# Loading the first slice of wq from ScalarE's queue, beside the first load of x

## The chip, the cores and the metric

The kernel runs on one core of a Trainium2 chip. Times are device microseconds (us) of one execution. The profile's "span", from the first to the last instruction, is in most runs 1.7 to 2.1 us shorter than that time. One of the first three runs of the kernel before took 343.19 us; it is a slow run and enters no comparison. TensorE is PE in the profile (PEld is its weight load), VectorE is DVE, ScalarE ACT, GpSimd POOL, SyncE SP; a q after a name is that engine's queue, which issues DMAs.

## The reference, cut to what matters

```python
x = A_x                                        # 2048 tokens x 640, bf16
g = sigmoid((x * gate_w).sum(-1, keepdims=True))
a = linear_attention(x @ wqkv, ...) @ wo       # 32 heads, phi(q), phi(k), sums over tokens
b = shift_mlp_block(x, w1, w2, w3, w4)
out = g * a + (1 - g) * b
```

Only the very beginning is touched by the change: x and the q columns of `A_wqkv` (called wq, 640 x 640) come in from memory, x is transposed, and the first four tiles of q are computed.

## The kernel before: the parts that matter

wq is cut into five slices of 128 rows (160 KB each), one per step of the contraction. Every load of the start-up is on SyncE, in this order:

```python
dma_in(x_tok[:, 0:2, :], ..., "x01")           # 320 KB: tokens 0-255
dma_in(x_tok[:, 2:4, :], ..., "x23")           # 320 KB: tokens 256-511
for k in range(KD):                            # KD = 5
    load_wq(k)                                 # 160 KB each
for k in range(KD):
    dma_in(wkg[:, k, 0:D], ..., "wk%d" % k)
...                                            # gate weights, the rest of x
```

TensorE begins with matmuls on a tile of ones, which do nothing but keep it at work, then transposes x, then streams q through four tiles:

```python
NWARM = 5
NWARM2 = 2
...
addA(("warm",), 0.0, lambda: warmup(NWARM, 427.0))
for i in range(4):
    addA(("tx", i), 0.28, lambda i=i: t_x(i))  # 5 transposes of one x tile, copied to xT
    if i % 2:
        addA(("warm", i), 0.0, lambda: warmup(NWARM2, 300.0))
addA(("q", 3), 5.44, q_four)                   # needs wq slice 0 first, then 1, 2, ...
addA(("k", 0), 1.36, k_first)
```

A helper works out all waits from what each operation reads and writes; each engine then runs its own list in order.

## Time and profile before

| | before |
|---|---|
| time, median of three runs | 267.33 us (fast runs 266.66 and 267.33) |
| span of the profiled run | 265.2 us |
| TensorE busy | 260.8 us, 98% |
| first x transposes start | 3.92 us |
| first wq matmul starts | 7.28 us |

The page's busy line of TensorE, and the engines of the chain of waits that ended last:

```profile
PE 260.8 (98%) x1729; PEld 137.3 (52%) x1729; DVE 146.3 (55%) x242; ACT 107.9 (41%) x218; POOL 91.8 (35%) x148
...
PE 98%; DVE 0%; POOL 0%; issue 0%; POOLq 0%
```

TensorE is both the busiest engine and the chain. The waits view of TensorE (engine, line, releaser; us in total, times, longest) has a single entry in the whole run, the start itself:

```profile
engine line waited for: us in total, times, longest us
PE ps L831 <- POOL ones_c L665: 1.6, 1, 1.6
```

The start-up in the timeline (start, duration, engine, line, operation, tiles, count, and in brackets the idle time before it with what ended it):

```profile
0.79 1.28 ACT L662 ACT_TABLE_LOAD   x1 [0.79 <-PEq L1226]
...
0.80 0.96 SPq L283 DMA_DIRECT2D x_tok<-in_A_x_dram  x2
...
1.59 2.31 PE L831 MATMUL ps<-ones_c 128*128 128x512 bf16 x5 [1.59 <-POOL ones_c L665]
...
1.81 2.36 SPq L283 DMA_DIRECT2D wq<-in_A_wqkv_dram  x5
...
3.91 0.99 PEld L617 LDWEIGHTS ps<-ident,x_tok 128*128 128x128 bf16 x10 [0.92 <-DMA x_tok<-in_A_x_dram]
3.92 1.25 PE L617 MATMUL ps<-ident,x_tok 128*128 128x128 bf16 x10
...
4.96 1.06 PE L831 MATMUL ps<-ones_c 128*128 128x512 bf16 x2
...
6.85 0.59 PE L831 MATMUL ps<-ones_c 128*128 128x512 bf16 x2
...
7.28 0.38 PE L853 MATMUL ps<-wq,xT 128*128 128x512 bf16 x1
```

SyncE issues the two x loads from 0.80 and the wq slices from 1.81. The warm-up matmuls end at 3.90, the transposes start at 3.92, and their weight loads waited for x_tok until 3.91: the first x load lands just there. The first wq matmul comes at 7.28, behind transposes and two more pairs of warm-up matmuls. wq slice 0 was issued at 1.81 and landed 3.7 to 3.9 us later (the range of the five slices in the source view), near 5.6, so it had over 1.5 us to spare.

The clock of TensorE shows in the weight loads and in the matmuls: the pair of warm-up matmuls at 4.96 takes 1.06 us, the same pair at 6.85 takes 0.59; single weight loads take 0.15 us before and 0.10 after. The switch from slow to full is at about 6.9 us. The page's row of granted clock does not show it; it is 9 everywhere.

Packets of the DMA queues between 1.8 and 3.4 us (packets, MB, share of the 16 engines' time). The first x load has 256 rows of 1280 bytes, and by the packet counts of these queues 16 more small packets at its end, 272 in all; wq slice 0 has 128 + 16 = 144:

```profile
q1 hardware_dynamic: 313, 0.38, 89.3%
```

By 3.4 us more packets have passed than the first x load has. (The 16 engines are not in step, so a few of them belong to the second.)

### The profile page before, as it was taken

The numbers are of one execution on the slowest core, as the hardware profiler recorded it, in microseconds if no ns is written. First come the engines' busy times: TensorE is split into PE (matmuls) and PEld (weight loads), VectorE is DVE, ScalarE is ACT, GpSimd is POOL, SyncE is SP. The second block draws the span as 40 slices with busy tenths as digits, with TensorE's granted clock in tenths as the row PEclk, the third lists the DMA queues.
The fourth block names the chain that finished last, engine by engine and source line by source line (L and its number), as shares of the span: only waits on it lengthen the run. The fifth ranks groups of instructions, "written<-read, shape, count | busy, mean of one in ns | idle before, by whom it ended". The sixth has DMA issues, their size and how long they took to land.

```text
span 265.2 us, 4339 instructions
## 1 busy us (share of the span) xinstructions
PE 260.8 (98%) x1729; PEld 137.3 (52%) x1729; DVE 146.3 (55%) x242; ACT 107.9 (41%) x218; POOL 91.8 (35%) x148
## 2 busy tenths in 40 slices
PE   7999999999999999999999999999999999999995
PEld 4555555555555555554445545545454455545553
DVE  0487877899903797999786986321212121122232
ACT  2486767742365757775651211212321312121000
POOL 4003995859874025688820204000120011021020
PEclk9999999999999999999999999999999999999999
DMA  7675899543568995256466831120000200002011
GB/s 224 221 100 140 184 175 150 174 102 22 104 124 114 304 371 70 48 99 64 63 124 124 103 68 30 31 95 2 0 0 6 95 0 0 2 0 101 0 49 49
DMA packets 50355, 24.77 MB, mean 93 GB/s; under 512 B 41756, under 2 KB 48925, under 8 KB 50336
## 3 DMA queue, kind: packets, MB, share of 16 engines
q1 hardware_dynamic: 49184, 21.23, 37.6%
q0 software_dynamic: 1152, 3.28, 5.4%
q8 instruction: 13, 0.21, 0.3%
q14 instruction: 6, 0.05, 0.1%
HBM read 12.04 MB, written 2.62 MB: 55 GB/s over the span
## 4 chain that ended last, share of the span: by engine, by line
PE 98%; DVE 0%; POOL 0%; issue 0%; POOLq 0%
PE ps L606 61%; PE ps L1100 21%; PE ps L783 8%; PE ps L853 2%; PE ps L831 1%; PE ps L1082 1%; PE ps L1022 1%; PE ps L617 1%; PE ps L939 1%; PE ps L854 1%; DVE x_tok L645 0%; POOL ones_c L665 0%; POOLq L1226 0%
## 5 line engine op out<-in xcount | busy, mean ns | idle before, releaser
L662 ACT ACTIVATE h2T<-ps 128x512 bf16<-128x512 f32 x52 | 31.0, 597 | 83.8 <-PE ps L606 83.7
L606 PE MATMUL ps<-xnT,w_58 128*128 128x512 bf16 x260 | 60.9, 379 | 0.0
L1100 PE MATMUL ps<-w_84,h2T 128*128 128x512 bf16 (+1 forms) x416 | 58.8, 299 | 0.0
L628 POOL TENSOR_SCALAR abx<-x_tok,stg 128x640 f32<-128x640 bf16 x16 | 13.9, 874 | 107.4 <-DVE x_tok L645 71.2
L1100 PEld LDWEIGHTS ps<-w_84,h2T 128*128 128x128 bf16 x416 | 32.7, 98 | 27.8 <-issue 1.3
L645 DVE SCALAR_TENSOR_TENSOR x_tok<-ps,stg,abx 128x640 bf16<-128x640 f32 (+2 forms) x17 | 14.3, 844 | 51.7 <-PE ps L1100 51.7
L606 PEld LDWEIGHTS ps<-xnT,w_58 128*128 128x128 bf16 x260 | 24.1, 98 | 24.8 <-issue 1.0
L645 DVE SCALAR_TENSOR_TENSOR abx<-ps,stg,abx 128x640 f32<-128x640 f32 x16 | 14.1, 882 | 27.9 <-PE ps L606 24.9
L662 ACT ACTIVATE Er<-ps 128x640 bf16<-128x640 f32 x32 | 22.4, 704 | 13.7 <-PE ps L606 8.8
L662 ACT ACTIVATE hsT<-ps 128x512 bf16<-128x512 f32 (+1 forms) x32 | 18.9, 593 | 14.6 <-PE ps L606 14.3
L661 ACT ACTIVATE junk<-x_tok 128x640 bf16<-128x640 bf16 x32 | 23.6, 736 | 2.0 <-DVE x_tok L643 1.7
L606 PE MATMUL ps<-M_sb,pqnT 128*128 128x512 bf16 (+1 forms) x160 | 24.1, 299 | 0.0
L606 PE MATMUL ps<-xnT,w_59 128*128 128x512 bf16 x100 | 23.9, 379 | 0.0
L783 PE MATMUL ps<-pk_tok,x_tok 128*128 128x512 bf16 (+1 forms) x160 | 23.9, 299 | 0.0
L606 PE MATMUL ps<-w_60,hsT 128*128 128x512 bf16 (+1 forms) x160 | 23.7, 299 | 0.0
L606 PE MATMUL ps<-wkg,xT 128*128 128x512 bf16 (+1 forms) x150 | 22.6, 299 | 0.0
L606 PEld LDWEIGHTS ps<-w_60,hsT 128*128 128x128 bf16 x160 | 13.3, 98 | 12.1
L606 PEld LDWEIGHTS ps<-M_sb,pqnT 128*128 128x128 bf16 x160 | 13.2, 98 | 12.1 <-issue 0.6
L628 POOL TENSOR_SCALAR xn<-x_tok,st_54 128x640 bf16<-128x640 bf16 x16 | 17.5, 1097 | 4.5 <-DMA xnT<-xn 4.4
L606 PE MATMUL ps<-wq,xT 128*128 128x512 bf16 (+1 forms) x120 | 18.3, 299 | 0.0
L628 POOL TENSOR_SCALAR xn<-x_tok,st_55 128x640 bf16<-128x640 bf16 x16 | 16.2, 1024 | 5.0 <-DMA xnT<-xn 4.6
L628 DVE TENSOR_SCALAR Er<-Er 128x640 bf16<-128x640 bf16 x32 | 12.0, 375 | 10.3 <-ACT Er L662 10.2
(74 smaller groups left out, 266.9 us busy)
## 6 DMA issues: line engine op xcount, KB each, us to landing
w_58<-in_B_w_dram SPq DMA_DIRECT2D x1, 2160.0 KB, 8.5
w_84<-in_B_w_dram SPq DMA_DIRECT2D x1, 2080.0 KB, 14.1
x_tok<-in_A_x_dram SPq DMA_DIRECT2D x3, 640.0 KB, 5.9
out_dram<-x_tok SPq DMA_DIRECT2D x3, 640.0 KB, 3.3
wq<-in_A_wqkv_dram SPq DMA_DIRECT2D x5, 160.0 KB, 3.8
wkg<-in_A_wqkv_dram SPq DMA_DIRECT2D x5, 160.0 KB, 4.1
wv<-in_A_wqkv_dram POOLq DMA_DIRECT2D x1, 800.0 KB, 5.9
wo_aug<-in_A_wo_dram POOLq DMA_DIRECT2D x5, 150.0 KB, 5.1
```

Of the source, the lines that this page charges most:

```text
L606: ins = e.matmul(out_ap, l, r, start=(i == 0), stop=(i == n - 1))
L617: ins = e.transpose(o, s_, ident[:])
L628: return engf(lambda e: e.tensor_scalar(out_ap, in_ap, s1, s2, op0, op1), rd, [out_ap], cost=cost)
L645: return dve(lambda e: e.scalar_tensor_tensor(out_ap, in0, scalar, in1, op0, op1), rd, [out_ap], cost=cost)
L661: return act(lambda e: e.activation(out_ap, in_ap, func, bias=bias, scale=scale, accum_out=accum), rd, wr, cost=cost)
L662: return act(lambda e: e.activation(out_ap, in_ap, func, bias=bias, scale=scale), rd, wr, cost=cost)
L783: ins = e.matmul(o, l, r, start=(t0 + q_ == 0), stop=(t0 + q_ == NT - 1))
L831: ins = e.matmul(ps[:, b, :], ones_c[:, 0:128], ones_c[:, 128:640], start=True, stop=True)
L853: e.matmul(ps[:, b, 0:512], l, w[:, k, 0:512], start=(k == 0), stop=(k == KD - 1))
L854: return e.matmul(ps[:, b + 1, 0:n2], l, w[:, k, 512:512 + n2], start=(k == 0), stop=(k == KD - 1))
L939: ins = e.matmul(o, l, r_, start=st_, stop=sp_, skip_group_check=True)
L1100: ins = e.matmul(o, l, r, start=False, stop=(i == KFF - 1))
```

## The change

The intent is to have the first wq slice early: its load is given to ScalarE's queue, which is free at the start, beside the first x load. The other slices stay behind x on SyncE.

```diff
+    sch.dma("act", wq[:, 0, :], A_wqkv[0:128, 0:D], "wq0")
     dma_in(x_tok[:, 0:2, :], x2[0:256, :]..., "x01")
...
     dma_in(x_tok[:, 2:4, :], x2[256:512, :]..., "x23")
-    for k in range(KD):
+    for k in range(1, KD):
         load_wq(k)
```

The instruction lists of TensorE, VectorE and GpSimd are the same in both kernels; only the two queues differ.

## The prediction

> **What bounds the kernel now.** TensorE: the page's busy table gives PE 260.8 us of a 265.2 us span (98%), and the chain that ended last is 98% PE. The waits view lists one PE wait in the whole run: 1.6 us for the ones tile of the warm-up matmuls.
>
> In the timeline, five warm-up matmuls end at 3.90. The first x transposes start at 3.92; the weight-load lane waited 0.9 us for the x_tok load until 3.91. This load (x01, 320 KB) is issued at 0.80 and lands after 3.1 us, at 3.9: it lands just as the warm-up ends, with no slack. x23 lands near 4.8 (issued about 1.28, 3.5 us; from the two-load median 3.3), used at 5.39 to 5.81. wq0 is issued at 1.81 and lands 3.7 to 3.9 us later, about 5.6. Its first matmul is at 7.28, right behind transposes and warm-ups in PE order: about 1.6 us of slack. No wait for wq appears.
>
> **What the change does.** It removes one issue (0.43 to 0.48 us) from SyncE, so x23 is unaffected and wq1 onward is issued about 0.48 us earlier. It adds one issue ahead of ScalarE's table load (0.79, 1.28 us long); ScalarE then idles 3.1 us until 5.20, so this is free. Nothing else changes order. wq0 itself should land about 1 to 1.3 us earlier (near 4.4), which nobody was waiting for: worth 0.
>
> The cost: wq0 now starts beside x01. The Trainium skill, "DMA: Bandwidth & Descriptors", section "Issuing engines are not separate DMA queues", says both queues end on the same 16 engines and interleave. The DMA view agrees that there is no spare room: share 84% from 1.59 to 3.92, then about 100% at 333 to 350 GB/s. wq0's 160 KB at 350 GB/s is 0.47 us. x01 has twice wq0's bytes, so with fair alternation x01 finishes after all or most of wq0: x01 lands an estimated 0.3 to 0.5 us later, 4.2 to 4.4. PE gets a gap of about 0.4 us before the first transposes. x23 moves as much, still before its use.
>
> **What of it is critical.** All of that gap, less one thing. PE runs at half clock until about 6.9 (weight loads 152 ns, later 98; warm-ups 427 ns apart, then 215). If the clock rises at a fixed time, as the skill's "TensorE: Matmul & The Clock Gate", Part 1, describes (a free-running activity window of about 3.4 us), work pushed past 6.9 runs twice as fast: a 0.4 us gap costs an estimated 0.2 us. If the rise slides with the gap, it costs 0.4; if the gap spoils a window, up to 1.7 (half of 3.4).
>
> **Predicted.** Fast runs of before are 266.66 to 267.33. I expect +0.1 to +0.5 us, +0.25 central: 267.35 us, 8 in 10 between 266.6 and 268.4. Faster by over 2%: 0.01; within 2%: 0.97; slower by over 2%: 0.02.
>
> **What would show it.** (1) First x transposes start 0.3 to 0.5 us later, with a PE wait on the x_tok load. (2) wq0 lands at 4.2 to 4.6, 1 us or more before its first matmul. (3) First wq matmul at 7.4 to 7.8. (4) Table load starts later by about 0.5, the first ScalarE copy still waits for PE. (5) Then a constant shift to the end; no new PE wait.
>
> **What would make it wrong.** ScalarE's queue starts late, so x01 goes first undisturbed: no change. The descriptor generation of both queues is shared and x01 waits longer: +0.5 or more. The clock rise moves by a whole window: -1 to +1.7 us. Run-to-run spread (0.7 us) exceeds the effect.

## The result, and the profile after

| | before | after |
|---|---|---|
| median of 6 runs | 267.0 us (the slow one among them; the five fast runs 266.66 to 267.33) | 268.53 us (267.95 to 269.51) |
| span of the profiled run | 265.2 us | 266.8 us |
| first x transposes start | 3.92 us | 4.68 us |
| clock of TensorE rises, by the weight loads | 6.9 us | 9.3 us |

The ratio is 1.0061, 95% interval 1.0039 to 1.0084. Ratios here are the mean time of one kernel's fast runs over that of the other's in the same rounds, so they are not quite the ratio of the medians. The kernel became 0.6% slower, about 1.6 us: still "the same" at 2%, but clear of noise, and above the range of the prediction.

The page's lines again, and TensorE's waits:

```profile
PE 261.6 (98%) x1729; PEld 137.5 (52%) x1729; DVE 145.7 (55%) x242; ACT 107.9 (40%) x218; POOL 91.7 (34%) x148
...
PE 97%; DMA 1%; DVE 0%; issue 0%
```

```profile
PE ps L832 <- POOL ones_c L665: 1.6, 1, 1.6
PE ps L617 <- DMA x_tok<-in_A_x_dram: 0.8, 1, 0.8
```

A second wait has come: 0.8 us for x. The DMA is now part of the chain. The timeline:

```profile
0.79 0.42 ACTq L283 DMA_DIRECT2D wq<-in_A_wqkv_dram  x1
...
0.80 0.97 SPq L283 DMA_DIRECT2D x_tok<-in_A_x_dram  x2
1.24 1.28 ACT L662 ACT_TABLE_LOAD   x1 [1.24 <-PEq L1227]
...
1.59 2.31 PE L832 MATMUL ps<-ones_c 128*128 128x512 bf16 x5 [1.59 <-POOL ones_c L665]
...
4.67 0.98 PEld L617 LDWEIGHTS ps<-ident,x_tok 128*128 128x128 bf16 x10 [1.68 <-DMA x_tok<-in_A_x_dram]
4.68 1.25 PE L617 MATMUL ps<-ident,x_tok 128*128 128x128 bf16 x10 [0.78 <-DMA x_tok<-in_A_x_dram]
...
8.49 0.63 PE L854 MATMUL ps<-wq,xT 128*128 128x512 bf16 x1
...
9.03 0.15 PEld L855 LDWEIGHTS ps<-wq,xT 128*128 128x128 bf16 x1
...
9.38 0.10 PEld L854 LDWEIGHTS ps<-wq,xT 128*128 128x128 bf16 x1 [0.20 <-issue]
```

The lines answer to those of before. ScalarE issues wq0 at 0.79, a hair before SyncE's x at 0.80; its table load slips from 0.79 to 1.24, which nobody feels. The warm-up ends at 3.90 as before, but x lands later: transposes at 4.68. The first wq matmul moves from 7.28 to 8.49. And the clock rises late: weight loads are still 0.15 us at 9.03 and 0.10 from 9.38.

The DMA queues between 1.8 and 3.4 us:

```profile
q10 hardware_dynamic: 141, 0.16, 60.3%
q1 hardware_dynamic: 111, 0.14, 24.7%
```

Queue 10 is ScalarE's. It has moved 141 of wq0's 144 packets by 3.4 us. SyncE's queue has moved 111, where it had moved 313 before; together the two queues moved 61 packets fewer than the one queue before, about 0.2 us of work at the 64 packets per 0.2 us of the kernel before near 3 us. These two counts could still come from turn-taking. The start decides it. From 1.8 to 2.2 us queue 10 alone moved packets (39), and from 2.2 to 2.6:

```profile
q10 hardware_dynamic: 27, 0.03, 48.9%
q1 hardware_dynamic: 8, 0.01, 10.6%
```

That is 66 against 8. The later overlap is one of engines that are not in step. The packed trace holds the small packet that ends each engine's share of a load: taken in order, x's came 0.68 us after wq0's on 14 of the 16 engines. At the 0.052 us per packet of e7_cols (0.834 us for 16 rows there) this is 13 of x's 16 rows per engine; turns of one row each would have left 8. So wq0 mostly went first. It landed 3.1 us after its issue, at 3.9 us, and was then used at 8.49.

**Where the 1.6 us come from.** Until the rise TensorE works at half speed (in the chain of waits two warm-up matmuls count 0.85 us before it and 0.43 after). So a delay in that stretch costs half its length, and each microsecond by which the rise comes later costs half a microsecond. Starting useful work 4.68 - 3.92 = 0.76 us later costs 0.38 us; the rise 9.3 - 6.9 = 2.4 us later costs 1.2 us. Together 1.58 us, against 266.8 - 265.2 = 1.6 us of span. From there on the run is only shifted: the group of three k tiles starts at 15.70 in place of 14.09, the first wo load is issued at 50.1 in place of 48.5, the last store at 264.4 in place of 262.8, each 1.6 us later.

So there are two questions: why x came 0.76 us late and not the expected 0.3 to 0.5, and whether the gap caused the late rise or the late rise was chance.

### The profile page after: what moved, and what is told of

Its sections match the earlier page's. It is cut to its first block, busy times and chain, and to the rows that moved or that the text cites. A ratio compares the mean times of both kernels' runs of the same rounds, so it can differ in the third digit from the quotient of the medians.

```text
span 266.8 us, 4339 instructions
## 1 busy us (share of the span) xinstructions
PE 261.6 (98%) x1729; PEld 137.5 (52%) x1729; DVE 145.7 (55%) x242; ACT 107.9 (40%) x218; POOL 91.7 (34%) x148
## 4 chain that ended last, share of the span: by engine, by line
PE 97%; DMA 1%; DVE 0%; issue 0%
PE ps L606 61%; PE ps L1101 21%; PE ps L784 8%; PE ps L854 2%; DMA x_tok<-in_A_x_dram 1%; PE ps L1083 1%; PE ps L1023 1%; PE ps L617 1%; PE ps L832 1%; PE ps L940 1%; PE ps L855 1%; DVE x_tok L645 0%
## 5 line engine op out<-in xcount | busy, mean ns | idle before, releaser
L628 POOL TENSOR_SCALAR xn<-x_tok,st_54 128x640 bf16<-128x640 bf16 x16 | 17.5, 1095 | 6.9 <-DMA xnT<-xn 6.8
L628 POOL TENSOR_SCALAR xn<-x_tok,st_55 128x640 bf16<-128x640 bf16 x16 | 16.8, 1058 | 5.1 <-DMA xnT<-xn 4.6
```

Source lines behind the costliest of these rows:

```text
L628: return engf(lambda e: e.tensor_scalar(out_ap, in_ap, s1, s2, op0, op1), rd, [out_ap], cost=cost)
```

## The experiments

Main theory: (1) wq0, issued first, goes ahead of x in the DMA engines; (2) the gap that this leaves in TensorE's work puts off the rise of its clock, which costs more than the gap. Rivals: the late rise is a chance of phase (of how the timing of the clock happens to stand when the kernel starts); the second queue costs by itself, through the table load or through sharing; only bytes count.

Twelve runs were made, of eleven kernels (e10 is e4 once more), all with correct results. Their times are set against the kernel before in the same session, whose own median is given, because it differs a little from session to session.

| kernel | median, before in that session | ratio, 95% interval | first x transposes start |
|---|---|---|---|
| three warm-up matmuls (e1_gap) | 267.98, 267.13 | 1.0029, 1.0008 to 1.005 | 3.90 |
| changed, seven warm-up matmuls (e2_fill) | 266.87, 267.13 | 0.9999, 0.9978 to 1.0019 | 4.89 |
| changed, wq0 issued at 2.68 (e3_late) | 266.91, 267.13 | 0.9991, 0.9973 to 1.0009 | 3.80 |
| wq0 first on SyncE (e4_spfirst) | 267.58, 267.13 | 1.0022, 0.999 to 1.0054 | 4.82 |
| before, dummy of 16 KB on ScalarE (e5_small) | 267.36, 266.77 | 1.0025, 1.0006 to 1.0043 | 4.22 |
| changed, 64 rows on ScalarE (e6_rows) | 266.34, 266.77 | 0.9987, 0.9969 to 1.0005 | 4.15 |
| changed, half rows on ScalarE (e7_cols) | 267.37, 266.77 | 1.0043, 1.0013 to 1.0074 | 4.51 |
| before, no warm-up pairs (e8_lean) | 266.55, 266.77 | 0.9999, 0.9979 to 1.0019 | 4.03 |
| changed, wq0 issued at 1.56 (e9_mid) | 266.7, 266.25 | 1.0022, 0.999 to 1.0053 | 3.77 |
| e4 once more, one look (e10_spagain) | 267.49, 266.25 | none | 4.21 |
| a try at a faster start (e11_try) | 266.85, 266.25 | 1.0018, 0.9986 to 1.005 | 4.74 |
| four warm-up matmuls (e12_gap4) | 266.78, 266.96 | 0.9987, 0.9974 to 1.0 | 3.61 |

### Is it the gap? A gap alone, and the change without its gap

The first takes two dummy matmuls away from the kernel before and leaves all loads as they were. TensorE idles, but nothing useful starts later.

```diff
-    NWARM = 5
+    NWARM = 3
```

> Kernel before with three warm-up matmuls in place of five, queues untouched. TensorE then idles about 0.85 us (3.05 to 3.9) before the first transposes, which start at the same 3.9 as before: no useful matmul is delayed. Main theory (a gap in TensorE's work puts off the rise of its clock): the rise (weight loads going from 0.15 to 0.10 us) moves from 6.9 to 8.5-10, and the span grows by half of that move, +0.8 to +1.5 us. Rival (the later rise in the changed kernel was chance of phase, or came from the DMA traffic): rise stays at 6.9 +- 0.5 and the time is that of before within 0.3 us.

```profile
1.58 1.46 PE L831 MATMUL ps<-ones_c 128*128 128x512 bf16 x3 [1.58 <-POOL ones_c L665]
...
3.90 1.25 PE L617 MATMUL ps<-ident,x_tok 128*128 128x128 bf16 x10 [0.85 <-DMA x_tok<-in_A_x_dram]
...
7.29 0.15 PEld L853 LDWEIGHTS ps<-wq,xT 128*128 128x128 bf16 x1 [0.27 <-issue]
...
7.71 0.10 PEld L854 LDWEIGHTS ps<-wq,xT 128*128 128x128 bf16 x1 [0.28 <-issue]
```

The transposes start at 3.90, as in the kernel before, after a gap of 0.85 us. The weight loads are still slow at 7.29 and fast at 7.71. The time is 1.0029 of before (1.0008 to 1.005), about 0.8 us more, by doing less. In its one profile the span grew by only 0.4 us with the rise near 7.7, 0.8 later: half of the move, as the sum above has it, though less of a move than the 8.5 to 10 expected of it; the other runs' spans go up to 266.7, against 264.4 to 265.8 for the kernel before in that session. A gap of this length costs time that no delayed work explains. (The six times show this, not the one profile: e12_gap4 below had its rise at 7.6 almost without a gap.)

The second keeps the changed loads, with x as late as there, but adds two warm-up matmuls so that TensorE is hardly idle (0.1 us in the profile, from 4.75 to 4.89).

```diff
-    NWARM = 5      # changed kernel
+    NWARM = 7
```

> Changed kernel with seven warm-up matmuls in place of five, so that they last until about 4.75, past the landing of the first x load at 4.63: x is as late, but TensorE has no gap. Main theory: the clock rises near 6.9 again (6.4 to 7.4), the useful chain starts 0.85 us later on the slow clock, and the total is +0.3 to +0.5 us over before, not the +1.6 of the changed kernel. Rival (the gap does not matter): rise near 9.3 and +1.6 us as in the changed kernel.

```profile
1.58 3.17 PE L832 MATMUL ps<-ones_c 128*128 128x512 bf16 x7 [1.58 <-POOL ones_c L665]
...
4.89 0.56 PEld L617 LDWEIGHTS ps<-ident,x_tok 128*128 128x128 bf16 x10 [1.04 <-DMA x_tok<-in_A_x_dram]
...
6.88 0.38 PE L854 MATMUL ps<-wq,xT 128*128 128x512 bf16 x1
```

x landed even later here, and transposes started at 4.89. Yet their ten weight loads took 0.56 us, not 0.99: the clock had risen already by about 4.9, earlier than the 6.4 to 7.4 expected. The time is that of before (0.9999), not the 0.3 to 0.5 us above it that were expected; the 0.43 us that two more slow warm-up matmuls should cost is within the interval. This run and the changed kernel differ in nothing but the filling of the gap, and the 1.6 us are gone: the six spans are 264.8 to 265.7 us here and 266.2 to 267.5 in the changed kernel. Chance of phase, with the gap playing no part, is ruled out by the two runs together.

Phase does play a part, though. The Trainium skill, "TensorE: Matmul & The Clock Gate", Part 1 ("What's actually happening"), says that the clock follows activity in a free-running window of 3413 ns that is not reset when a kernel starts. That agrees with what is seen here: with no gap, the rise was at 6.9 in one profile and before 4.9 in another, and the spans of the kernel before range from 264.0 to 266.1 us over the sessions. If all of this came from the rise, it would be a range of an estimated 4 us in it.

The other profiles bear out the sum by which the 1.6 us were split. Take 265.2 us and add half of what the transposes start later than 3.92 and half of what the rise (read from the spacing of the matmuls, 0.43 us slow and 0.22 fast) comes later than 6.9. For e1_gap (rise 7.7) this gives 265.6 us, e4_spfirst (7.9) 266.1, e5_small (6.9) 265.4, e7_cols (5.3) 264.7, e9_mid (5.7) 264.5, e10_spagain (7.6) 265.7 and e12_gap4 (7.6) 265.4; each measured span is within 0.1 us of it. The rises also sort by the gap: with gaps of at most 0.14 us (seven profiles) they lie between 4.7 and 7.6, with 0.25 to 0.61 (four) between 5.0 and 7.6, with 0.78 to 0.92 (three: the changed kernel, e1_gap, e4_spfirst) between 7.7 and 9.3.

How long may a gap be? The last run halves it.

```diff
-    NWARM = 5
+    NWARM = 4
```

> Kernel before with four warm-up matmuls in place of five: a gap of about 0.4 us (3.47 to 3.9) before the first transposes, half of that with three, and again no useful matmul delayed. If every gap puts off the clock rise (any idle restarts the count), the rise moves to 7.3 or later and the time by +0.5 to +1.0 us, as with three. If only a gap that is a large enough part of a window does (profiles with gaps of 0.25, 0.31 and 0.61 us had their rise 0.9 to 3.3 us after the gap, less than a whole window of 3.4; those with 0.78 and 0.85 had 3.6 and 4.6), the time is that of before within 0.4 us.

```profile
3.60 0.98 PEld L617 LDWEIGHTS ps<-ident,x_tok 128*128 128x128 bf16 x10 [1.04 <-DMA x_tok<-in_A_x_dram]
```

There is no cost (0.9987, 0.9974 to 1.0). But in the profile x happened to land early, at 3.6, so the gap there was about 0.1 us and not 0.4; the run says that four matmuls are enough on the average, and gives no limit for a gap. That stays open. (In the text of the expectation the two last numbers are in the wrong order: 4.6 us belongs to the gap of 0.78, 3.6 to that of 0.85, or 3.8 by the spacing of the matmuls. It also leaves out e4_spfirst, whose rise came only about 3.0 us after its gap of 0.92; so no rule of a whole window after a large gap follows.)

### Is it the second queue, or the place of wq0 ahead of x?

In this run ScalarE issues wq0 only after a mask that GpSimd makes, at 2.68.

```diff
-    sch.dma("act", wq[:, 0, :], ..., "wq0")
...
-    aselect(mask[0:120], mask_t[0:120], ...)
+    late = aselect(mask[0:120], mask_t[0:120], ...)
+    sch.dma("act", wq[:, 0, :], ..., "wq0", deps=[late])
```

> Changed kernel, but ScalarE's wq0 load waits for the GpSimd mask (about 2.65), so that it starts when the first x load is nearly through. Main theory (only the overlap with the first x load costs; the move to the other queue is free): x lands at 3.9 to 4.0, wq0 near 6.2, before its first matmul at 7.28; no TensorE gap; time of before within 0.3 us. Rival (having wq0 on ScalarE's queue costs by itself, by the delayed table load or by the other slices coming earlier on SyncE): slower than before by 0.5 us or more.

The transposes started at 3.80, and the time is that of before (0.9991). The table load went to 3.12, and the first wq matmul waited 0.47 us for wq0 at 7.28: with an early clock rise in that profile, before 5.7, wq0 was just on the critical path, at no visible cost. The move to ScalarE's queue is free; the moment is what costs.

The next puts wq0 ahead of x on SyncE's own queue, one queue for all, in place of the load on ScalarE:

```diff
+    dma_in(wq[:, 0, :], A_wqkv[0:128, 0:D], "wq0")   # on SyncE
     dma_in(x_tok[:, 0:2, :], ..., "x01")
```

> wq0 first on SyncE's own queue, then the first x load: same bytes ahead of x, one queue. If bytes (and one issue slot of 0.46 us) are all there is, x lands 0.45 to 0.5 us later than before, near 4.4, gap about 0.5 us. If two queues beside each other cost more than their bytes (descriptor supply in the start-up, unfair turns), x lands earlier here than in the changed kernel (4.63). If it lands at 4.6 or later, the second queue adds nothing. By the gap theory the clock rise is late here too (8.5 to 10): +1 to +1.6 us over before.

```profile
0.80 0.40 SPq L283 DMA_DIRECT2D wq<-in_A_wqkv_dram  x1
...
4.82 1.25 PE L617 MATMUL ps<-ident,x_tok 128*128 128x128 bf16 x10 [0.92 <-DMA x_tok<-in_A_x_dram]
```

x came at least as late as with two queues, at 4.82. So no unfair sharing between two queues is needed to explain the delay: 160 KB in front of x will do, together with x's own issue, which came 0.45 us later here (1.25 in place of 0.80). The time expected, 1 to 1.6 us over before, was missed: the ratio is 1.0022 with an interval that holds 1. But the times of this kernel spread from 266.28 to 269.09 us, and one profile is thin, so it was looked at once more:

> The single-queue kernel (wq0 first on SyncE) once more, for one more landing of x: its times spread from 266.3 to 269.1 and its one profile had x at 4.82. If the delay of x there is steady, 4.6 to 4.9 again; if it varies from run to run, which would explain the spread, it may be anywhere from 4.3.

Now the transposes started at 4.21, a delay of 0.29 us and not 0.9. The same loads in the same order land 0.6 us apart from run to run. In the kernel before's order of loads, the starts seen are 3.90, 3.92, 4.03 and, with four warm-up matmuls, 3.61. A single landing therefore settles nothing finer than about 0.3 us. The two, 0.29 and 0.90 us, lie on either side of the 0.45 to 0.5 us expected.

Then wq0 on ScalarE was issued between the two: after the ones tile, at 1.56, when SyncE had issued both x loads but none of their bytes had moved yet.

```diff
-    memset(pool, ones_c[:], 1.0)
+    ones_ev = memset(pool, ones_c[:], 1.0)
+    sch.dma("act", wq[:, 0, :], ..., "wq0", deps=[ones_ev])
```

> Changed kernel, but ScalarE's wq0 load waits for the ones tile (about 1.55), so SyncE has issued both x loads before it, while the first x load is still moving. If the part of x's delay beyond wq0's bytes (0.78 against 0.47 us) comes from wq0 being set up first, at 0.79, it is gone here: the first packets of x go as in the kernel before, and only turn-taking is left: x lands 0 to 0.45 us later than 3.9. Rival (two queues side by side are slow however they start): x lands at 4.6 again. By the clock theory the time is before +0 to +0.9.

```profile
0.80 0.97 SPq L283 DMA_DIRECT2D x_tok<-in_A_x_dram  x2
1.56 0.37 ACTq L283 DMA_DIRECT2D wq<-in_A_wqkv_dram  x1
...
3.77 1.25 PE L617 MATMUL ps<-ident,x_tok 128*128 128x128 bf16 x10
```

```profile
q1 hardware_dynamic: 328, 0.40, 86.2%
q10 hardware_dynamic: 1, 0.00, 0.2%
```

This is the run that tells most about the queues. wq0 was issued 0.77 us later than in the changed kernel, and by 3.4 us its queue had moved one packet, while SyncE's had moved 328. The transposes started at 3.77, no later than in the kernel before. The bulk of wq0 moved after 4.2 us (87 packets from 4.2 to 4.6), when SyncE's queue had moved 513 of the 544 packets of its two x loads, which had been issued earlier. With wq0 issued at 0.79, the counts at the same moment were 141 and 111. Whichever load's issue ended first was served first, although they sat on two queues (in the changed kernel ScalarE's issue ended at 1.21, SyncE's first at 1.25); rows of the two mostly did not alternate on an engine. The time is 1.0022 of before with an interval that holds 1 (one of its six runs, 268.61 us, had a span of only 265.7, so its excess is not in the kernel's execution).

### How much is it the bytes?

A dummy load on ScalarE, of as many rows as wq0 but a tenth of the bytes, into a place that is used only much later:

```diff
+    sch.dma("act", M_sb[:, 0, 0:64], A_wqkv[0:128, 0:64], "dummy")   # kernel before
```

> Kernel before, all of wq on SyncE as it was, and beside the first x load a dummy load on ScalarE of as many rows as wq0 (128) but 128 bytes each, 16 KB in all, into a place that is free until later. If x is delayed by the bytes beside it, 16 KB at 350 GB/s is 0.05 us: x lands at 3.9 to 4.0, time of before. If it is delayed by rows (turns taken by each packet, or the making of descriptors for two queues in the start-up), x lands 0.4 us or more later (4.3 to 4.7), with a TensorE gap and +0.5 to +1.6 us.

```profile
q1 hardware_dynamic: 253, 0.31, 61.7%
q10 hardware_dynamic: 144, 0.02, 6.8%
```

By 3.4 us SyncE's queue had moved 253 packets, 60 fewer than before. The transposes started at 4.22, 0.3 us late, and the time is 1.0025 of before (1.0006 to 1.0043). Bytes alone would give 0.05 us of delay. So a small load beside x is not free either: neither theory was right, since x was late by less than the 0.4 us of one and more than the 0.05 of the other.

Half of wq0 on ScalarE, once as 64 rows and once as 128 half rows; the other half goes on SyncE ahead of wq1:

```diff
-    sch.dma("act", wq[:, 0, :], A_wqkv[0:128, 0:D], "wq0")
+    sch.dma("act", wq[0:64, 0, :], A_wqkv[0:64, 0:D], "wq0a")       # e6_rows
+    sch.dma("act", wq[:, 0, 0:320], A_wqkv[0:128, 0:320], "wq0a")   # e7_cols
```

> Changed kernel with only the upper 64 partitions of wq0 on ScalarE (64 rows of 1280 bytes, 80 KB); the other 64 go on SyncE ahead of wq1. Bytes and rows are both half of the changed kernel's, so both theories expect half of its delay of x: landing near 4.25 (4.1 to 4.4). A fixed cost of having any second queue in the start-up would leave it near 4.6.

> Changed kernel with only the first 320 columns of wq0 on ScalarE (128 rows of 640 bytes, 80 KB). Bytes theory: as the 64-row run, x lands near 4.25. Rows theory: as the changed kernel, 4.6.

With 64 rows the transposes started at 4.15, and the kernel was no slower than before (0.9987); ScalarE's queue had moved 54 packets by 3.4 us and SyncE's 291. But this run did not put the half of wq0 ahead of x. Its issue on ScalarE took 0.55 us in place of 0.42,

```profile
0.79 0.55 ACTq L283 DMA_DIRECT2D wq<-in_A_wqkv_dram  x1
```

so it ended at 1.34, after SyncE's first at 1.25, and by 2.6 us SyncE's queue had moved 99 packets and ScalarE's none. That x started within the 4.1 to 4.4 expected says nothing of bytes or rows, and why it was late at all was not found. With 128 half rows they started at 4.51, and the kernel was slower (1.0043; the profile is of the fastest of its four runs, with an early rise, and does not show the loss); the counts were 144 and 128:

```profile
GB/s 16 96 112 64 112 16 0 0 0 0 0 0 0 0 0 0 0 0 32 16 0 16 64 32 112 272 224 272 304 432 400 304 352 448 432 352 352 416 416 480
...
q10 hardware_dynamic: 144, 0.08, 36.8%
q1 hardware_dynamic: 128, 0.16, 27.5%
```

Here the DMA engines began no packet for about 0.5 us (the zeros in the first line, in slices of 0.04 us from 1.8), with both loads issued and waiting. The sum of starts (4.22 for 16 KB, 4.51 for 80 KB, 4.68 for 160 KB, each of 128 rows) fits a fixed 0.3 us and 160 KB at 350 GB/s, but with the scatter that e4 and e10 showed this is an estimate from three single profiles, not a law. The packed trace shows what the slow start is made of: single packets that take far longer than the usual 0.055 us, up to 0.54 us in the kernel before, 0.86 in the changed one, 0.94 in e7_cols (five such packets begin just ahead of the zeros) and 1.34 in e2_fill. Why they do was not found; it differs from profile to profile.

### Tries at something faster

If wq0 has time to spare, the warm-up pairs in front of it are perhaps not needed:

```diff
-        if i % 2:
-            addA(("warm", i), 0.0, lambda: warmup(NWARM2, 300.0))
```

> Kernel before without the two pairs of warm-up matmuls after the first and second transposes. wq0 lands near 5.6 in before and its first matmul runs at 7.28, behind those pairs, so if the slack is real the first wq matmul moves to about 6.0 to 6.4. The four matmuls are worth 0.86 us at full clock: time -0.4 to -0.9 us against before. Rival (the pairs are needed to keep the clock rise early, or to cover waits for xT and later x): no gain, or a new wait of TensorE for xT or x_tok around 16 to 18 us.

The two waits of TensorE's weight loads that are new with it:

```profile
PEld ps L853 <- DMA wq<-in_A_wqkv_dram: 0.7, 2, 0.5
PEld ps L606 <- DMA xT<-x_tok: 0.5, 1, 0.5
```

The first wq matmul moved to about 6.0, as expected, but the time did not change (0.9999). TensorE now waited for wq, and later for the transposed x. The group of three k tiles started 0.99 us earlier than before (13.10 against 14.09; that profile also had an early clock), the first wo load 0.7 us earlier. The rest of the gain was given back in between. In the kernel before, the spare time of wq0 is taken up by work that hides later loads.

The last try sets the ones tile on VectorE, drops only the second pair, moves the small gate load from SyncE to ScalarE after its first copy, and starts with seven warm-up matmuls:

```diff
-    memset(pool, ones_c[:], 1.0)
+    memset(dve, ones_c[:], 1.0)
-    NWARM = 5
+    NWARM = 7
-        if i % 2:
+        if i == 1:
...                      # gate load: from SyncE to ScalarE
```

> A try at a faster start-up, built on kernel before: the ones tile is set by VectorE (idle then) in place of GpSimd, so the warm-up and with it the clock rise begin about 0.5 us earlier (seven warm-up matmuls to reach x at 3.9); the second pair of warm-up matmuls is dropped; the 1 KB gate load goes from SyncE to ScalarE after its first copy, so that the third x load is issued 0.48 us earlier. Hoped: -0.25 (clock) -0.4 (pair) = -0.4 to -0.9 us. If the later xT transposes bound the chain at 17 to 24 us, as they did when both pairs were dropped, it gains only 0 to -0.3.

```profile
1.02 0.70 DVE L665 MEMSET ones_c<- 128x768 bf16 x1 [1.02 <-PEq L1227]
...
1.78 3.17 PE L832 MATMUL ps<-ones_c 128*128 128x512 bf16 x7 [1.78 <-DVE ones_c L665]
...
4.74 1.27 PE L617 MATMUL ps<-ident,x_tok 128*128 128x128 bf16 x10
```

It missed. VectorE began its memset at 1.02 and took 0.70 us, so the warm-up began at 1.78, not 0.5 us earlier but 0.2 later, and seven slow matmuls kept TensorE from x until 4.74. The time is 1.0018 of before, no difference that can be told. No kernel beat the kernel before clear of noise.

## Why the prediction was wrong

- **What bounds the kernel, and the worth of wq0: right.** TensorE was the chain, wq0 had time to spare (3.9 to 8.49 after the change), and its earlier landing brought nothing. The only effect was a later x, then a gap, then a constant shift to the end; the table load was free. All of this is in the trace.
- **"With fair alternation x01 finishes after all or most of wq0: x01 lands an estimated 0.3 to 0.5 us later": this step failed in its premise and in its size.** The start of the transposes moved by 0.76 us in the changed kernel's profile, and by 0.97 us with the same loads in e2_fill. The counts (66 packets against 8 up to 2.6 us, and 1 against 328 up to 3.4 when wq0 was issued 0.77 us later) show that the order of issue decided, across the queues. The wrong premise cost nothing by itself: x has twice wq0's bytes, so with fair turns too it would have ended behind all of wq0, 0.47 us late. What was missing is what came on top, about 0.3 us. Some 0.2 us of it is a slower start of the DMA engines (252 packets by 3.4 us in place of 313), and a 16 KB load also came with such a loss (SyncE's queue 60 packets short). How large that part is on the average, and why, stays open.
- **"If the clock rises at a fixed time ... a 0.4 us gap costs an estimated 0.2 us": this step failed, and it cost more.** The central figure took the rise as fixed. It came 2.4 us later, 1.2 of the 1.6 us. This is the step that decided: with the measured 0.76 us and a fixed rise the cost would have been 0.38 us, within the +0.1 to +0.5 us expected. The prediction had "if the gap spoils a window, up to 1.7" as its worst case and gave it little weight. A gap alone (e1_gap) costs about 0.8 us with no work delayed, and filling the gap (e2_fill) takes the loss away. With a gap of 0.4, as predicted, the rise might have stayed among the usual ones: it did in the four profiles with gaps of 0.25 to 0.61. So the error in the first step may have brought on the second; no run had a gap of 0.4 to show it. Nor is the rise at one time without a gap (4.7 to 7.6 in seven profiles); the 6.9 was one draw.
- **The checks in the prediction.** First transposes 0.3 to 0.5 us later: 0.76. wq0 lands at 4.2 to 4.6: 3.9. First wq matmul at 7.4 to 7.8: 8.49. Table load later by about 0.5, free: 0.45, free. Constant shift, no other new wait: so it was.
- The predicted 267.35 us and the range 266.6 to 268.4 were both too low; the median is 268.53. "Within 2%" was right.

## What to carry to other kernels

Before moving a load to an idle queue, look who waits for it, and which load is the first that the busiest engine waits for: anything issued before that one, on whichever queue, can delay it, and issued a little later it cost nothing that these runs can tell. At the start of a kernel, keep TensorE at work until its first data surely lands; a gap there can put off its full clock and cost more than its own length. And where times of one kernel scatter by more than the effect, look for the state that differs from run to run (here the moment of the clock's rise) before believing a single profile.

## What the Trainium skill lacked or had wrong

- "DMA: Bandwidth & Descriptors", sections "Queues, rings and completion order" and "Issuing engines are not separate DMA queues": it says that an engine goes round-robin between queues, a whole packet of some 9 to 17 descriptors at a time, and that DMAs of different issuers interleave. This agrees with these traces if each load is one such packet on each engine: wq0's 144 packets of the profile are 9 per engine, x01's 272 are 17. (So what the profile calls a packet would be the page's descriptor; this is inferred, not tested.) What is missing is that small loads are then served whole, and in which order: the one whose issue ended first, 66 against 8 packets up to 2.6 us with ScalarE's issue ending 0.04 us ahead, and 1 against 328 up to 3.4 us with it 0.68 us behind.
- The same page, "Specifications" and "Latency and other measured facts", gives about 0.6 us to the first byte for loads issued from SyncE and ScalarE. This agrees with these traces when it is counted from the end of the issue: in the kernel before the issue of the first x load ran from 0.80 to 1.25 and the first packet began at 1.89, 0.64 us later; counted from the start of the issue it is 1.09. The page does not say from where to count. The engines then took until about 2.6 us to get to speed; no page has this slow start, or the 0.5 us in which no packet began in e7_cols.
- "TensorE: Matmul & The Clock Gate", Part 1: it names a busy window of about 3.4 us but not how much idle time a window may hold. Here a gap of 0.85 us cost about 0.8 us by itself; with four warm-up matmuls (a gap of 0.1 us in the profile) there was no cost.
